# Gates of the later columns behind the fourth chunk, low words on two engines and other block sizes, in an mLSTM with a bilinear MLP

## The chip, the cores and the metric

The kernel runs on one core of a Trainium2 chip. The metric is device time in microseconds (us). Engines are named as in the profile: PE (TensorE) does matmuls, ACT (ScalarE) activations and copies, DVE (VectorE) elementwise work, POOL (GpSimd) elementwise work on SBUF, and SP (SyncE) issues all DMAs, from one queue in order.

## The reference

An mLSTM runs over 4 batches x 8 heads, 768 steps and a head dimension of 40. Its output, 3072 tokens of 320 values, goes through a bilinear MLP with d_ff = 1536. All inputs are float32 but the three MLP matrices, which are float64.

```python
for t in range(S):
    m_new = np.maximum(f_gate[:, :, t] + m, i_gate[:, :, t])
    f_stab = np.exp(f_gate[:, :, t] + m - m_new)
    i_stab = np.exp(i_gate[:, :, t] - m_new)
    m = m_new
    C = f_stab[:, :, None, None] * C + i_stab[:, :, None, None] * np.einsum('bhd,bhe->bhde', vt, kt)
    n = f_stab[:, :, None] * n + i_stab[:, :, None] * kt
    h_tilde = np.einsum('bhde,bhe->bhd', C, qt)
    denom = np.maximum(np.abs(np.einsum('bhd,bhd->bh', n, qt)[:, :, None]), 1.0)
    y[:, :, t] = 1.0 / (1.0 + np.exp(-o_gate[:, :, t])) * h_tilde / denom
x = y.transpose(0, 2, 1, 3).reshape(B * S, H * D)
out = (x @ w_a) * (x @ w_b) @ w_out
```

## The kernel before

**Chunks.** The 768 steps are cut into 6 columns of 128, and a chunk is one column of one batch: 24 chunks, ordered by column and then batch, so chunks 0 to 3 are the first column. In a chunk the recurrence becomes attention: S = k q^T per head, times a matrix E of decays (the masked exp of gate sums), times v (pV); plus, from the second column on, the state of the batch times q (pI); then a division by the denominator and a product with the output gate (stage_f), and a transpose (stage_d, `pX`) that yields x for the MLP, split into a high and a low part (`xh`, `xl`). stage_u adds the chunk's k and weighted v (`vw`, made by weigh on POOL) to the state `cst` of its batch.

**Gates.** first_gates handles the first 128 columns (chunks 0 to 3); their E comes from one-hot matmuls (begin_e). later_gates handles the other 640: a running maximum (scan, L218), three adds, a prefix sum for each column (L228), a table `tab` with three rows of columns, its write to DRAM (`g_dram`, L235), transposes on PE (`ptg`) into `gtab`, exps on ACT (L263), and `dec`, the decay from column to column. load_g reads a chunk's sums back from `g_dram`, broadcast to 128 partitions (`gbc`); stage_e masks it on POOL (L409) and takes eight exps on ACT (L416). In this kernel the weights `vw` of chunks 0 to 3, too, are read from `gtab`.

**MLP weights.** The float64 words are loaded as they are (`raw`, 32 stages), and each is turned into float32 and then into a high and a low float32r part: high on ACT (L342), low words on DVE for stages 0 to 4 and on ACT for stages 5 to 31 (L350, L352), join on DVE (L357), lead_part on ACT (L370), low_part on DVE (L376). The conversions of stages 5 to 31 run beside block 0. An up-projection step of index ff needs all stages up to 8*(ff//3)+4.

**Blocks.** The MLP runs over blocks of two or three chunks (`sizes`). Each of a block's 12 steps has 16 up matmuls (`pu`, L747), 256 or 384 wide, evacuated by ACT and DVE (L754 to L759), and, two steps later, three down matmuls a chunk (`pd`, L719). Three PSUM buffers hold `pu`. Beside block kb the attention of the next block's chunks is emitted; run_block paces it. Blocks 0 and 1 are ordered by a scheduler that simulates the engines; from block 2 on the order of PE and SP is that of the code, and the other engines are scheduled. Chunks up to 5 run as early_chunk, the later ones as late_chunk with bf16 triples and the DMA transposes of stage_a. Before block 0 a hand-written order on PE, ACT, DVE and SP does chunks 0 and 1 and stages 0 to 4.

**Loads.** SP issues q, k, v of a chunk into one of three buffers (`qk`, `va`), so chunk 3 uses the buffers of chunk 0 and has to wait for that chunk's stage_u. Each DMA also waits for the one eight issues earlier.

The rule that puts an instruction behind others is `with tc.issue_after(x)`. Three of the places that the change touches are these:

```python
        with tc.issue_after(start["dve"]):
            nc.vector.tensor_tensor_scan(m, f, i, gm[:, P - 1:P], op0=ALU.add, op1=ALU.max)
    sizes = [2, 2, 3, 3, 3, 3, 3, 2, 3]
        if x < NF0:
            nc.vector.tensor_scalar(W.bitcast(U32), lo, 2.0 ** -29, 7.0, op0=ALU.mult, op1=ALU.min)
```

## Time and profile before

| | before |
|---|---|
| median of 3 runs (lowest to highest) | 552.54 us (552.09 to 553.96) |
| profiled execution, its own time | 555.06 us |
| its span | 553.28 us |
| mean granted clock of PE | 0.975 |
| block 0's outputs copied on ACT (L729) | 102.91 us |
| block 1's | 151.41 us |
| block 2's | 211.37 us |
| HBM read / written | 41.11 / 5.97 MB |

Times within the execution count from the start of the span. A row of groups gives line, engine, operation, output <- inputs, shape, count | busy us, mean ns of one | idle time of the engine just before it and who ended most of it. A row of stretches gives, for each engine, its busy time in the stretch and (in brackets) its instructions, then the clock that was granted to PE, the mean busy share of the DMA engines, and GB/s. A row of waits reads: engine, instruction <- engine and line waited for: us in total, times, the longest. A row of the timeline has start, duration, engine, line, operation. A row of the chain of waits has start, us, engine, tile, line and count.

### The profile page before, as it was taken

The numbers are of one execution on the slowest core, as the hardware profiler recorded it, in microseconds if no ns is written. First come the engines' busy times: TensorE is split into PE (matmuls) and PEld (weight loads), VectorE is DVE, ScalarE is ACT, GpSimd is POOL, SyncE is SP. The second block draws the span as 40 slices with busy tenths as digits, with TensorE's granted clock in tenths as the row PEclk, the third lists the DMA queues.
The fourth block names the chain that finished last, engine by engine and source line by source line (L and its number), as shares of the span: only waits on it lengthen the run. The fifth ranks groups of instructions, "written<-read, shape, count | busy, mean of one in ns | idle before, by whom it ended". The sixth has DMA issues, their size and how long they took to land.

```text
span 553.3 us, 12427 instructions
## 1 busy us (share of the span) xinstructions
PE 529.7 (96%) x4810; PEld 504.1 (91%) x4810; DVE 407.9 (74%) x940; ACT 233.8 (42%) x559; POOL 126.5 (23%) x185
## 2 busy tenths in 40 slices
PE   9668999999999999999999999999999999899997
PEld 6568899998999999999899999899999999799997
DVE  6887868769799885997589895887777568744342
ACT  5699986434433451343342341542331514210111
POOL 2003534543143223133043122133030202100000
PEclk9687899999999999999999999999999999999999
DMA  9999814778639756569558564957555745100001
GB/s 174 307 253 318 146 28 101 161 139 154 109 97 186 153 95 129 107 110 188 92 130 163 117 113 122 157 104 155 84 130 78 134 77 131 21 1 25 1 0 37
DMA packets 198679, 66.77 MB, mean 121 GB/s; under 512 B 184252, under 2 KB 191900, under 8 KB 198620
## 3 DMA queue, kind: packets, MB, share of 16 engines
q1 hardware_dynamic: 198620, 65.98, 58.2%
q8 instruction: 38, 0.62, 0.5%
q14 instruction: 21, 0.17, 0.1%
HBM read 41.11 MB, written 5.97 MB: 85 GB/s over the span
## 4 chain that ended last, share of the span: by engine, by line
PE 74%; ACT 10%; DVE 5%; DMA 5%; issue 4%; SPq 2%; POOL 1%; POOLq 0%; ACTq 0%; DVEq 0%
PE pu L747 40%; PE pd L719 20%; PE pV L523 3%; DMA osig<-in_o_gate_dram 2%; PE pS L471 2%; PE pU L547 2%; ACT qks L342 1%; ACT L167 1%; ACT w L370 1%; PE pS L821 1%; PE pX L633 1%; PE pV L873 1%; SPq L160 1%; ACT cw L352 1%; ACT gbc L416 1%
## 5 line engine op out<-in xcount | busy, mean ns | idle before, releaser
L747 PE MATMUL pu<-xh,w 128*128 128x384 f32 (+1 forms) x1080 | 281.3, 327 | 2.1 <-ACT gbc L787 0.7
L747 PE MATMUL pu<-xl,w 128*128 128x384 f32 (+1 forms) x648 | 210.3, 326 | 1.0 <-DVE xl L639 1.0
L747 PEld LDWEIGHTS pu<-xh,w 128*128 128x128 f32 x1080 | 193.9, 192 | 4.0 <-ACT xh L637 1.0
L719 PE MATMUL pd<-w,gh 128*128 128x320 f32 x576 | 132.2, 316 | 2.8 <-ACT gh L757 2.8
L747 PEld LDWEIGHTS pu<-xl,w 128*128 128x128 f32 x648 | 124.6, 192 | 1.8 <-DVE xl L639 1.3
L719 PEld LDWEIGHTS pd<-w,gh 128*128 128x128 f32 x576 | 98.0, 191 | 3.5 <-ACT gh L757 3.2
L755 DVE TENSOR_TENSOR g<-pu,g 128x384 f32<-128x384 f32 (+1 forms) x108 | 54.7, 507 | 58.8 <-PE pu L747 55.5
L754 ACT COPY g<-pu 128x384 f32<-128x384 f32 (+1 forms) x92 | 40.4, 439 | 116.0 <-PE pu L747 114.7
L719 PE MATMUL pd<-w,gl 128*128 128x320 f32 x288 | 89.3, 319 | 0.0
L416 ACT ACTIVATE gbc<-gbc,gtab 128x128 f32<-128x128 f32 x160 | 49.2, 391 | 21.5 <-POOL gbc L409 19.8
L458 POOL TENSOR_TENSOR vr<-va 128x336 f32<-128x336 f32 x18 | 14.1, 782 | 188.7 <-PE pV L523 178.3
L719 PEld LDWEIGHTS pd<-w,gl 128*128 128x128 f32 x288 | 53.8, 191 | 0.2
L759 DVE TENSOR_TENSOR gl<-g,gh 128x384 fp32r<-128x384 f32 (+1 forms) x92 | 50.8, 552 | 1.6
L757 DVE CAST gh<-g 128x384 fp32r<-128x384 f32 (+1 forms) x96 | 34.2, 356 | 1.6
L478 ACT CAST pb<-gbc 128x512 bf16<-128x512 f32 x36 | 22.2, 616 | 29.4 <-DVE gbc L476 29.4
L530 DVE TENSOR_TENSOR num<-pV,num 128x336 f32<-128x336 f32 x18 | 9.1, 505 | 31.7 <-PE pV L523 31.6
L565 ACT CAST cb<-cst 128x168 bf16<-128x168 f32 x18 | 6.0, 332 | 54.5 <-DMA gbc<-g_dram 21.4
L610 POOL TENSOR_TENSOR osig<-osig,den 128x320 f32<-128x320 f32 x22 | 17.7, 804 | 41.1 <-DVE den L605 22.1
L409 POOL TENSOR_SCALAR_AFFINE_SELECT gbc<-gbc 128x1024 f32<-128x1024 f32 x20 | 23.6, 1182 | 14.6 <-DMA gbc<-g_dram 12.3
L476 DVE TENSOR_TENSOR gbc<-pS,gbc 128x512 f32<-128x512 f32 x36 | 24.5, 681 | 3.3 <-PE pS L471 3.3
L523 PEld LDWEIGHTS <-pb 128*128 128x128 bf16 x576 | 23.0, 96 | 4.1 <-DVE pb L482 1.8
L523 PE MATMUL pV<-va,pb 128*128 128x42 bf16 x288 | 25.0, 183 | 1.6 <-DVE pb L482 1.6
(131 smaller groups left out, 809.1 us busy)
## 6 DMA issues: line engine op xcount, KB each, us to landing
gbc<-g_dram SPq DMA_DIRECT2D x20, 512.0 KB
qk<-in_q_dram SPq DMA_DIRECT2D x24, 160.0 KB
qk<-in_k_dram SPq DMA_DIRECT2D x24, 160.0 KB
va<-in_v_dram SPq DMA_DIRECT2D x24, 160.0 KB
osig<-in_o_gate_dram SPq DMA_DIRECT2D x24, 160.0 KB
raw<-in_moe_w_out_dram SPq DMA_DIRECT2D x12, 320.0 KB
out_dram<-o SPq DMA_DIRECT2D x24, 160.0 KB
raw<-in_moe_w_a_dram SPq DMA_DIRECT2D x8, 384.0 KB
```

The lines of the kernel that those rows point to most:

```text
L409: nc.gpsimd.affine_select(E, E, pattern=[[0, H], [1, P]], compare_op=ALU.is_ge, fill=-1e30, base=0, channel_multiplier=-1,)
L416: nc.scalar.activation(E[:, h], E[:, h], AF.Exp, bias=beta[:, h:h + 1])
L476: nc.vector.tensor_tensor(E, pS, E, op=ALU.mult)
L478: nc.scalar.copy(pb[:, 0], E)
L523: nc.tensor.matmul(pv[:, h], pb[i][:, h % HH, :], vb[j][:, h], start=(x == 0), stop=(x == len(terms) - 1),)
L610: (nc.vector if n < NS else nc.gpsimd).tensor_tensor(yv, yv, den.unsqueeze(2).broadcast_to([P, H, D]), op=ALU.mult)
L719: nc.tensor.matmul(pd[t][:, 0:DM], a[:, cols], w, start=(ff == 0 and first), stop=(ff == NF - 1 and last),)
L747: up_in = nc.tensor.matmul(acc[j], a, r, start=(x == 0), stop=(x == len(terms) - 1),).ins
L754: (nc.vector.tensor_copy if kb > 0 and ff in [1, 2] else nc.scalar.copy)(g, acc[0])
L755: nc.vector.tensor_tensor(g, acc[1], g, op=ALU.mult)
L757: (nc.vector.tensor_copy if kb > 0 else nc.scalar.copy)(gh, g)
L759: (nc.gpsimd if kb * 12 + ff < 16 else nc.vector).tensor_tensor(gl, g, gh.bitcast(F32), op=ALU.subtract)
```

## The change

It has these parts:

- later_gates runs no longer at the start of the work beside block 0, but in early_chunk(3), behind that chunk's V, F, D and U. Its first scan follows the last low part (`after["dve"]`). It leaves out the first column, so `tab`, `gtab` and `g_dram` have five columns, and the exps of `gtab` become two.
- first_weights, new, makes the weights of chunks 0 to 3 in the hand-written part (an add on DVE, a transpose on PE, an exp on ACT into `w0tab`). weigh for chunks 0 and 1 follows there, and their stage_u comes first beside block 0.
- The low words of stages with an even number go to DVE, the odd ones stay on ACT.
- sizes is [2, 2, 2, 3, 3, 3, 3, 3, 3].
- The squash (sigmoid of the output gate) of batches 2 and 3 is emitted after the E of chunk 3. q and k of chunk 2 are loaded ahead of the weights of stages 9 to 12. The pace of run_block in block 0 has a lead of 8 units, and a conversion step is emitted every 3 units, not 4. The zeroing of `qks2` is split. The tile of `vw` shares its tag with `vr`.

```diff
+    w0tab = wpool.tile([P, BH], F32, name="w0tab")
...
-    sizes = [2, 2, 3, 3, 3, 3, 3, 2, 3]
+    sizes = [2, 2, 2, 3, 3, 3, 3, 3, 3]
...
+    def first_weights():
+        w0 = gf[:, 0:P]
+        nc.vector.tensor_scalar(w0, gb3[0][:, 1], gb3[0][:, 0, P - 1:], None, op0=ALU.add)
+        pw = ps_dn.tile([P, 512], F32, tag="pd2", name="pw")[:, 0:BH]
+        nc.tensor.transpose(pw, w0, ident[0:BH, 0:BH])
+        nc.scalar.activation(w0tab, pw, AF.Exp)
+
     def later_gates():
...
-        with tc.issue_after(start["dve"]):
+        with tc.issue_after(after["dve"]):
             nc.vector.tensor_tensor_scan(m, f, i, gm[:, P - 1:P], op0=ALU.add, op1=ALU.max)
...
-        with tc.issue_after(start["act"]):
-            nc.scalar.copy(G[:, 0], gb3[0][:, 0])
-            nc.scalar.copy(tab[BH:2 * BH, 0], gb3[0][:, 1])
...
-            nc.sync.dma_start(g_dram.rearrange("c g t -> g c t"), G)
+            nc.sync.dma_start(g_dram[1:].rearrange("c g t -> g c t"), G[:, 1:])
...
-        x = gtab[:, BH:].rearrange("p (c g) -> p c g", g=3 * BH)[:, :, 0:2 * BH]
+        nc.scalar.activation(a_col(1, 0, B), a_col(1, 0, B), AF.Exp)
+        x = gtab[:, 4 * BH:].rearrange("p (c g) -> p c g", g=3 * BH)[:, :, 0:2 * BH]
...
     def w_col(c, b):
-        return g_col(c, b, 1)
+        return g_col(c, b, 1) if c > 0 else w0tab[:, b * H:(b + 1) * H]
...
-        if x < NF0:
+        if x < NF0 or x % 2 == 0:
             nc.vector.tensor_scalar(W.bitcast(U32), lo, 2.0 ** -29, 7.0, op0=ALU.mult, op1=ALU.min)
         else:
             nc.scalar.activation(W.bitcast(U32), lo, AF.Copy, scale=7.499 * 2.0 ** -32)
...
                     high(x)
+                with tc.issue_after(start["dve" if x % 2 == 0 else "act"]):
                     low(x)
...
-        for x in qks2:
+        clear(qks2[0:2])
...
-        if n > NS:
+        if n > NS and n != NE:
             yield from stage_d(n - 1)
         aside("O", n)
+        if n == NE - 1:
+            yield from begin_c(n)
+            yield from stage_f(n)
+            yield from stage_d(n)
+            yield from stage_u(n)
+            yield from later_gates()
+            clear(qks2[2:4])
+            load_g(NE)
         yield from (begin_e if n + 1 < NE else stage_e)(n + 1)
+        if n == NS:
+            for b in range(NS, B):
+                squash(0, b, 1)
...
-        yield from begin_c(n)
-        yield from stage_u(n)
-        yield from stage_f(n)
+        if n != NE - 1:
+            yield from begin_c(n)
+            yield from stage_u(n)
+            yield from stage_f(n)
...
-        vw = apool.tile([P, H, DV], F32, tag="vw", name=f"vw{n}", bufs=1)
+        vw = apool.tile([P, H, DV], F32, tag="vr", name=f"vw{n}")
...
-        for x in range(5, 13):
+        for x in range(5, 9):
             fetch(x)
-        load(2)
+        load_qk(2)
+        for x in range(9, 13):
+            fetch(x)
+        load_v(2)
...
         run(E[1], 2)
+        first_weights()
         run(S_[1])
...
+        for n in range(NS):
+            weigh(n)
...
     def rest():
-        gates = later_gates()
-        for _ in range(2):
-            next(gates)
-            yield
-        yield from begin_a(NS)
-        yield from begin_e(NS)
-        yield from gates
         for n in range(NS):
-            weigh(n)
             yield from stage_u(n)
             if n == 0:
                 with tc.issue_after(issued["w"]):
                     load(NS + 1)
-        for b in range(2, B):
-            squash(0, b, 1)
-        load_g(NE)
+        yield from begin_a(NS)
+        yield from begin_e(NS)
         yield from attention()
...
-        acc = 0.0
+        lead_in = 8 if kb == 0 else 0
+        acc = -lead_in
...
-            if x % (4 if kb == 0 else 6) == 0:
+            if x % (3 if kb == 0 else 6) == 0:
                 next(conv, None)
-            acc += units / (total * (0.93 if kb < 2 else 0.88))
+            acc += (units + lead_in) / (total * (0.93 if kb < 2 else 0.88))
```

What the scheduler makes of it, at three places. Names carry the tile's number; the lines of the kernel after are shifted by some 5 to 25 against those before.

On ACT beside the start of block 0, before: L342 is high, L352 a low word, L370 a lead part, L754 and L757 evacuate `pu`, L787 is an exp of E, L167 the squash.

```order
L787 ACT_TABLE_LOAD
L787 ACTIVATE gbc_513<-pE_0_514 128x512
L167 ACT_TABLE_LOAD
L167 ACTIVATE osig_159<-osig_159 128x320
L787 ACT_TABLE_LOAD
L787 ACTIVATE gbc_513<-pE_1_535 128x512
L370 CAST w_588<-cw 128x384
L342 ACTIVATE qks_89<-raw_184 128x384
L167 ACT_TABLE_LOAD
L167 ACTIVATE osig_159<-osig_159 128x320
L757 CAST gh_0_502<-g_0_470 128x256
```

The same place on ACT in the changed kernel (L347 is high, L357 a low word, L375 a lead part, L775 and L778 evacuate `pu`, L808 is the exp of E, L168 the squash):

```order
L168 ACTIVATE osig_160<-osig_160 128x320
L357 ACTIVATE cw<-raw_181 128x384
L168 ACTIVATE osig_160<-osig_160 128x320
L375 CAST w_587<-cw 128x384
L347 ACTIVATE qks_89<-raw_193 128x320
L357 ACTIVATE cw<-raw_185 128x384
L778 CAST gh_1_565<-g_1_521 128x256
L775 COPY g_2_619<-pu_2_0_569 128x256
L808 ACT_TABLE_LOAD
L808 ACTIVATE gbc_604<-pE_0_605 128x512
L375 CAST w_669<-cw 64x384 x2
```

The two squashes stand ahead of the exps of E, so one table load is left of four; no further one comes until block 1.

On SP behind the last weight load, before: q of chunk 3 (`qk_80`), the write of the gate sums, then loads of chunks 3 to 5, k of chunk 3 among them, and the first `gbc`.

```order
L142 DMA qk_80<-in_q_dram 128x8x40
L235 DMA g_dram<-qks_92 32x6x128
L148 DMA va_86<-in_v_dram 128x8x40
L142 DMA qk_81<-in_q_dram 128x8x40
L142 DMA qk_80<-in_k_dram 128x8x40
L148 DMA va_87<-in_v_dram 128x8x40
L142 DMA qk_82<-in_q_dram 128x8x40
L180 DMA gbc_696<-g_dram 128x1024
```

The same place on SP in the changed kernel:

```order
L143 DMA qk_80<-in_q_dram 128x8x40
L143 DMA qk_80<-in_k_dram 128x8x40
L149 DMA va_86<-in_v_dram 128x8x40
L143 DMA qk_81<-in_q_dram 128x8x40
L149 DMA va_87<-in_v_dram 128x8x40
L143 DMA qk_82<-in_q_dram 128x8x40
L143 DMA qk_81<-in_k_dram 128x8x40
L143 DMA qk_82<-in_k_dram 128x8x40
```

k of chunk 3 follows its q. The gate sums and their first reading now stand 20 rows on, at the end of block 0, again on SP in the changed kernel (L751 writes block 0's outputs, L161 loads output gates of the second column):

```order
L240 DMA g_dram<-qks_92 32x5x128
L161 DMA osig_1475<-in_o_gate_dram 128x8x40 x2
L751 DMA out_dram<-o_0_1239 128x320
L751 DMA out_dram<-o_1_1242 128x320
L181 DMA gbc_1362<-g_dram 128x1024
L181 DMA gbc_1401<-g_dram 128x1024
```

Between the write and the first reading two loads and the two outputs of block 0 are queued.

On ACT around the exp of `gtab` (L263) and `dec` (L269), before, in the middle of block 0:

```order
L352 ACTIVATE cw<-raw_194 128x320
L263 ACT_TABLE_LOAD
L263 ACTIVATE gtab<-gtab 128x5x64
L269 ACTIVATE dec<-pdec 128x64
L352 ACTIVATE cw<-raw_198 128x384
L754 COPY g_3_742<-pu_3_0_691 128x256
```

And in the changed kernel, at the start of block 1 (L266 and L268 are the exps of `gtab`, L425 those of chunk 4's E and, in the last row, chunk 5's, L274 is `dec`):

```order
L266 ACTIVATE gtab<-gtab 128x32
L775 COPY g_0_1271<-pu_0_0_1247 128x256
L268 ACTIVATE gtab<-gtab 128x4x64
L425 ACTIVATE gbc_1362<-gbc_1362,gtab 128x128 x8
L274 ACTIVATE dec<-pdec 128x64
L168 ACT_TABLE_LOAD
L168 ACTIVATE osig_1475<-osig_1475 128x4x320
L775 COPY g_3_1410<-pu_3_0_1385 128x256
L425 ACT_TABLE_LOAD
L425 ACTIVATE gbc_1401<-gbc_1401,gtab 128x128 x8
```

The copy of block 1's fourth accumulator stands behind the exps of chunk 4's E, `dec` and the squash.

More of the change, by code (lines that the diff above doesn't have):

```diff
@@ L245, in later_gates @@
         nc.vector.tensor_tensor(
-            tab[2 * BH:], tab[BH:2 * BH], G[:, :, P - 1:P].broadcast_to([BH, NC, P]), op=ALU.add
+            tab[2 * BH:, 1:], tab[BH:2 * BH, 1:], G[:, 1:, P - 1:P].broadcast_to([BH, NC - 1, P]),
+            op=ALU.add,
         )
@@ L251, in later_gates @@
             n3 = NC // 2
-            for c in range(n3):
+            cs = range(max(half * n3, 1), (half + 1) * n3)
+            for x, c in enumerate(cs):
                 nc.tensor.transpose(
-                    pt[:, c * 3 * BH:(c + 1) * 3 * BH], tab[:, half * n3 + c, :],
-                    ident[0:3 * BH, 0:3 * BH],
-                )
-            n0, n1 = (BH, n3 * 3 * BH) if half == 0 else (0, (n3 * 3 - 1) * BH)
-            nc.vector.tensor_copy(
-                gtab[:, half * (n3 * 3 - 1) * BH:][:, 0:n1 - n0], pt[:, n0:n1]
-            )
+                    pt[:, x * 3 * BH:(x + 1) * 3 * BH], tab[:, c, :], ident[0:3 * BH, 0:3 * BH]
+                )
+            n1 = (len(cs) * 3 - half) * BH
+            nc.vector.tensor_copy(gtab[:, (3 * cs[0] - 1) * BH:][:, 0:n1], pt[:, 0:n1])
             yield
-        x = gtab[:, BH:].rearrange("p (c g) -> p c g", g=3 * BH)[:, :, 0:2 * BH]
+        nc.scalar.activation(a_col(1, 0, B), a_col(1, 0, B), AF.Exp)
+        x = gtab[:, 4 * BH:].rearrange("p (c g) -> p c g", g=3 * BH)[:, :, 0:2 * BH]
         nc.scalar.activation(x, x, AF.Exp)
@@ L270, in later_gates, with g_col @@
         yield
-    def g_col(c, b, x):
-        return gtab[:, (3 * c + x) * BH + b * H:][:, 0:H]
+    def g_col(c, b, x, nb=1):
+        return gtab[:, (3 * c + x) * BH + b * H:][:, 0:nb * H]
     def beta_col(c, b):
@@ L278, in w_col, with a_col @@
     def w_col(c, b):
-        return g_col(c, b, 1)
-    def a_col(c, b):
-        return g_col(c - 1, b, 2)
+        return g_col(c, b, 1) if c > 0 else w0tab[:, b * H:(b + 1) * H]
+    def a_col(c, b, nb=1):
+        return g_col(c - 1, b, 2, nb)
     def weight_stages():
@@ L393, in weights, with clear @@
                 yield x
-        for x in qks2:
+        clear(qks2[0:2])
+    def clear(tiles):
+        for x in tiles:
             for w in range(2):
@@ L621, in stage_d @@
     def stage_d(n):
-        s = st[n] if n < NS else st.pop(n)
+        s = st[n] if n < NE else st.pop(n)
         k_ = block[n]
```

## The prediction

> **What bounds the kernel now.** The page comes first: the busy shares and the granted clock over 40 slices of 13.8 us.
>
> ```profile
> PE 529.7 (96%) x4810; PEld 504.1 (91%) x4810; DVE 407.9 (74%) x940; ACT 233.8 (42%) x559; POOL 126.5 (23%) x185
> PEclk9687899999999999999999999999999999999999
> ```
>
> TensorE is busy for 96% of the span, so only time in which it idles or runs slowly can be won. The clock row says where the second kind lies: in the first six slices. The busy times by stretches, cut where the clock changes and where blocks end, give the sizes.
>
> ```profile
> core 0: us, PE busy (x) PEld busy (x) DVE busy (x) ACT busy (x) POOL busy (x), PEclk, DMA share, GB/s
> ...
> 22.25:71.80 49.55, 41.10 (x312) 37.69 (x313) 41.06 (x78) 46.89 (x110) 12.73 (x19) 0.78 0.93 233
> 71.80:102.90 31.10, 31.10 (x255) 29.34 (x254) 23.00 (x49) 22.22 (x57) 14.20 (x23) 1.00 0.38 79
> ...
> 102.90:151.40 48.50, 47.24 (x470) 45.28 (x470) 38.57 (x95) 19.99 (x57) 17.45 (x22) 1.00 0.76 145
> ...
> 211.40:274.30 62.90, 61.78 (x599) 58.73 (x598) 51.06 (x119) 23.53 (x58) 16.73 (x21) 1.00 0.67 131
> ...
> 456.10:500.70 44.60, 42.12 (x484) 41.16 (x483) 28.71 (x73) 11.77 (x30) 5.07 (x6) 1.00 0.20 48
> ```
>
> The first matmul of block 0 stands at 22.25 us. From there to 71.8 TensorE idles 49.55 - 41.10 = 8.45 us, and the mean clock of 0.78 takes up to 0.22 x 49.55 = 10.9 us more. After 71.8 the clock is full and TensorE has work almost without a gap. So 8.45 + 10.9 = 19.3 us is about all that this change can touch before the later blocks. Who holds TensorE there? ACT is busy 46.89 of 49.55 us. The waits of TensorE name ACT's casts and a load:
>
> ```profile
> PE pd L719 <- ACT gh L757: 2.8, 2, 1.7
> PE pT L808 <- DMA qk<-in_q_dram: 2.5, 1, 2.5
> ```
>
> ACT's groups while the weights of stages 5 to 31 are converted, 25.8 to 89.4 us, show what fills it.
>
> ```profile
> L370 ACT CAST w<-cw 128x384 fp32r<-128x384 f32 (+2 forms) x31 | 15.6, 502 | 4.6 <-DVE cw L357 4.5
> ...
> L352 ACT ACTIVATE cw<-raw 128x384 uint32<-128x384 uint32 (+1 forms) x27 | 14.0, 532 | 0.0
> ...
> L787 ACT ACT_TABLE_LOAD x2 | 2.6, 1283 | 0.0
> L167 ACT ACT_TABLE_LOAD x2 | 2.6, 1283 | 0.0
> L416 ACT ACTIVATE gbc<-gbc,gtab 128x128 f32<-128x128 f32 x8 | 2.5, 430 | 0.0
> ```
>
> **The change, part by part.** ACT first. 13 of the 27 low words leave it: 13 x 0.532 = 6.9 us. Five table loads stand in this stretch (two and two above, one for gtab's exps) and by the new order one is left: 4 x 1.28 = 5.1 us. The exps of chunk 4 (2.5 us) and the gates' small copies and exps (1.3 us) move behind the stretch. ACT's durations overlap by about a fifth where they stand side by side (the groups add up to 71 us in 58 us of busy time), so 10.7 us of ordinary work is worth 8.7, and with the loads 13.8 us. ACT idles 5.5 us there. Without idle time its last cast comes at 89.4 - 5.5 - 13.8 = 70 us instead of 89.4.
>
> VectorE takes the 13 low words and loses the gates.
>
> ```profile
> L376 DVE TENSOR_TENSOR w<-cw,w 128x384 fp32r<-128x384 f32 (+2 forms) x29 | 17.5, 618 | 1.3 <-ACT w L370 1.0
> L357 DVE SCALAR_TENSOR_TENSOR cw<-qks,cw 128x384 uint32<-128x384 uint32 (+1 forms) x27 | 16.8, 644 | 1.5 <-ACT cw L352 1.0
> ...
> L228 DVE TENSOR_TENSOR_SCAN qks<-one,qks 32x128 f32<-32x128 f32 x5 | 1.7, 389 | 0.0
> L218 DVE TENSOR_TENSOR_SCAN qks<-qks 32x640 f32<-32x640 f32 x1 | 1.5, 1542 | 0.0
> ...
> L222 DVE TENSOR_TENSOR qks<-qks 32x640 f32<-32x640 f32 x1 | 0.8, 815 | 0.0
> ```
>
> ```profile
> 22.29 0.36 DVE L350 TENSOR_SCALAR cw<-raw 128x384 uint32<-128x384 uint32 x1
> ```
>
> 13 x 0.36 = 4.7 us come. The gates go: 1.7 + 1.5 + five operations of 0.8 to 0.95 and two copies of 0.4, 8.1 us; with them some 3 us of chunk 4's attention. VectorE idles 13.5 us in the stretch now, so without idle time it would be through at 89.4 - 13.5 - 8.1 - 3 + 4.7 = 69.5 us. Both engines thus end near 70, each nearly full. Weights of the last up-projection steps are wanted three stages (5 us) earlier.
>
> Now TensorE. I follow the end T of block 0's last up-projection.
>
> ```profile
> 99.47 0.28 PE L747 MATMUL pu<-xl,w 128*128 128x256 f32 x1
> ```
>
> T is 99.75 before. The new order has less ahead of that point: chunk 4's S, I and transposes, the gate transposes, a chunk's U and X and 12 down matmuls come later. From the groups of TensorE, 22 to 102 us, and its pitch in the chain of waits:
>
> ```profile
> L821 PE MATMUL pS<-T,T 40*128 40x128 f32 x48 | 5.8, 285 | 0.0
> L808 PE MATMUL pT<-ident,qk 128*128 128x128 f32 x32 | 5.3, 293 | 2.6 <-DMA qk<-in_q_dram 2.5 <-DMA qk<-in_k_dram 0.2
> ...
> L547 PE MATMUL pU<-vw,qk 128*64 128x42 f32 x84 | 4.1, 249 | 0.0
> ...
> L842 PE MATMUL pI<-cst,T 40*128 40x42 f32 x16 | 2.2, 284 | 0.0
> ```
>
> ```profile
> 493.30 1.92 PE pu L747 x16
> ...
> 498.02 2.64 PE pd L719 x18
> ```
>
> A third of 5.8, three eighths of 5.3, a quarter of 4.1, all of 2.2, about 2 for gate transposes and X, and 12 x 0.147 = 1.8: 11 us, some 9.5 where the records' overlaps are taken off. This work is not saved, only done later. At equal work T before is 99.75 - 9.5 = 90.2 us.
>
> When does T come after? From TensorE: 77.5 us from 22.25 to T are 8.45 idle, 10.9 clock and 58.2 work; less 9.5 leaves 48.7. With half the clock loss (5.5) and a wait of 2 us for chunk 2's q, whose load moves ahead of five weight loads, T = 22.25 + 48.7 + 5.5 + 2 = 78.4. From the loads of chunk 3:
>
> ```profile
> 49.55 0.38 SPq L142 DMA_DIRECT2D qk<-in_q_dram  x1
> ```
>
> ```profile
> 56.72 0.68 SPq L142 DMA_DIRECT2D qk<-in_k_dram  x1
> ```
>
> ```profile
> 61.54 0.66 PE L808 MATMUL pT<-ident,qk 128*128 128x128 f32 x4 [0.16 <-DMA qk<-in_k_dram]
> ```
>
> k is issued at 56.72 and lands by 61.5; in the new queue it follows q at once, since U of chunk 0 no longer waits for the gate table, so about 51.7 and landed by 56.5. Behind its transposes stand 81 up matmuls of 0.12, 30 down of 0.147, two V (3.8), S, U and X (3): 21 us, T = 77.5 at full clock and 79.5 with one more slow stretch. I take **T = 79: a gain of 11.2 us**. Bounds: 76 if everything keeps pace, 85 if ACT and VectorE wait for each other at every stage.
>
> Then the gates, now ahead of chunk 4. The scan waits for the last low part; by VectorE's new order the five chunk scans come right behind the product of the last up step, at T + 2.4. SP's order is g_dram, two gate loads, block 0's two outputs, then chunk 4's gbc.
>
> ```profile
> 26.54 1.54 DVE L218 TENSOR_TENSOR_SCAN qks<-qks 32x640 f32<-32x640 f32 x1
> ```
>
> ```profile
> 51.79 0.43 SPq L235 DMA_DIRECT2D g_dram<-qks  x1
> ...
> 59.88 0.98 SPq L180 DMA_DIRECT2D gbc<-g_dram  x1
> ...
> 83.31 0.36 SPq L180 DMA_DIRECT2D gbc<-g_dram  x1
> ```
>
> ```profile
> 65.49 1.31 POOL L409 TENSOR_SCALAR_AFFINE_SELECT gbc<-gbc 128x1024 f32<-128x1024 f32 x1 [1.26 <-DMA gbc<-g_dram]
> ...
> 87.42 1.10 POOL L409 TENSOR_SCALAR_AFFINE_SELECT gbc<-gbc 128x1024 f32<-128x1024 f32 x1 [0.79 <-DMA gbc<-g_dram]
> ```
>
> ```profile
> 101.73 1.27 ACT L167 ACTIVATE osig<-osig 128x1280 f32<-128x1280 f32 x1
> ```
>
> Block 0's last 18 down matmuls, X and transposes end at T + 3.8, the outputs are issued at T + 5, gbc at T + 6.3. It lands after 4.1 us (83.31 to 87.42; 5.6 from 59.88), the mask takes 1.2, the exps 2.5: T + 14.2. ACT is in order: dec's exp, a table load of 1.28, the squash of 1.27 and only then the copy of pu of step 3, done at T + 17.3. TensorE reaches the matmul that needs this accumulator (64 + 8 up, 12 down, 3 us of small work) at T + 16.5. I charge **1.2 us**, between 0 (block 0's tail slower than that) and 11 (a rival below). E itself is wanted only some 8 us later, so the rest of the chain is covered; uncovered, its 14 us would count whole.
>
> Block sizes: matmul counts stay (three blocks of 2, six of 3). Three late chunks beside a block of 2 now fall to block 2. VectorE has 51.06 us in a full block, about 6 less beside a block of 2, 45 us, where such a block takes 44.6. I charge **1.0 us** (0 to 3). Block 7 is no longer such a block, and block 1 gets two chunks; their idle 1.3 and up to 2.5 us (some of it missing records) I credit with **0.5** (0 to 2). first_weights adds a small transpose, an add and an exp ahead of 22.25, beside idle time of TensorE: nothing, 0.4 at most. vw of chunks 0 to 3 runs on POOL earlier: nothing, since POOL is busy 12.73 of 49.55 us; its cover gone, 1.1 each.
>
> Sum: -11.2 + 1.2 + 1.0 - 0.5 = **-9.5 us**. The profiled execution took 555.06 us (span 553.28), 2.5 above the median of 552.54; its like would be 545.6, and the median 552.5 - 9.5 = **543.0 us**.
>
> **The clock.** The slow stretches are no plain answer to idling:
>
> ```profile
> 47.90:65.00 17.10, 14.56 (x148) 12.91 (x146) 14.97 (x27) 17.02 (x42) 5.99 (x8) 1.00 0.94 213
> 65.00:71.80 6.80, 6.80 (x40) 6.38 (x41) 5.98 (x14) 6.61 (x21) 3.97 (x5) 0.50 0.56 90
> ```
>
> Before 65.0 TensorE was 85% busy, and still the next 6.8 us ran at half clock. Hence I keep half the clock loss though the idle gaps shrink. The Trainium skill ("TensorE: Matmul & The Clock Gate", Part 1: The HAM clock gate) has the clock halved after an idle window of about 3.4 us and released after a busy one. By that rule a well-fed block 0 would run at full clock from about 31 us on. The trace agrees in the length of the stretches (6.8 is two such windows), not in the cause at 65.0.
>
> **The rivals.**
> - *The clock stays open after 31 us*: loss 4.3 instead of 5.5 and no second slow stretch behind k; T = 76.3, sum -12.2, **540**. For: fewer gaps. Against: the row at 65.0. 13%.
> - *VectorE becomes the bound of block 0*. Each stage goes ACT, VectorE, ACT, VectorE; joins and low parts took 0.62 to 0.64 us, over the 0.5 of their quick ones. If half of its 13.5 us of idle time stays, the last cast is at 76.5 and T near 83.5: sum -5, **547.5**. 17%.
> - *The gain is given back in blocks 1 and 2* by charges at their upper ends (some 4 + 3) on top of T = 83.5: **552**. 5%.
> - *Slower: the gate chain is exposed.* Before, scan to mask took 65.49 - 26.54 = 39 us, for gbc stood behind other loads. Starting at T - 7 and 3.8 us from mask to E, it would end at T + 36, where TensorE wants E at T + 24.8: 11 us of stall, and two slow windows (3.4): -11.2 + 11 + 3.4 + 1 - 0.5 = +3.7, **556**. It decides from a stall of 8 us. Against: its queue place is now close behind g_dram. 5%.
>
> **How the numbers follow.** The forecast (540.5 to 546) has 60%. The range of 538 to 550 takes in the first two rivals and leaves out 10 to 15%. A measurement of this kernel tells 0.3%, 1.7 us, from no change. Faster: 60 + 13 + 17 = 90%; same 5%; slower 5%.
>
> **What would show it.** Right: block 0's outputs copied on ACT near 84 us instead of 102.9; one table load for L787 there; the last weight cast near 70; a wait of about 1 us of TensorE for the copy of pu in block 1. Wrong: VectorE above 95% to 80 us with TensorE waiting for w; a PE wait for E of chunk 4; idle time of several us in block 2.

## The result, and the profile after

The kernel after takes 567.23 us (564.30 to 569.63, 4 executions) against 552.54: ratio 1.026, 95% interval 1.021 to 1.031. It is slower by 2.6%, where 543.0 us, faster by 1.7%, was forecast, and it lies outside the range of 538 to 550. The profiled execution took 566.81 us (span 565.0), so it stands for the median.

The first view is the page of the kernel after: TensorE's busy share, and the granted clock in 40 slices, here of 14.1 us.

```profile
PE 532.7 (94%) x4810; PEld 503.4 (89%) x4810; DVE 411.9 (73%) x954; ACT 224.1 (40%) x542; POOL 128.2 (23%) x185
PEclk9699899999899799999999999999999899999999
```

The share fell from 96% to 94%. Of the 6, 8, 7 and 8 in slices two to five a 6 and an 8 are left, as hoped, but there are new dents in slices eleven, fourteen and thirty-two, where the kernel before had none. The stretches say which blocks they are in (block 0 in three pieces, block 1, block 2, block 6; columns as in the prediction):

```profile
22.25:58.40 36.15, 29.19 (x254) 25.83 (x255) 28.75 (x60) 30.84 (x77) 5.78 (x7) 0.92 1.04 270
58.40:61.80 3.40, 3.40 (x18) 3.40 (x17) 1.03 (x2) 1.81 (x5) 2.05 (x3) 0.50 1.11 147
61.80:88.66 26.86, 25.07 (x202) 23.63 (x201) 25.70 (x56) 16.09 (x43) 10.16 (x16) 1.00 0.35 55
88.66:146.16 57.50, 54.11 (x449) 49.74 (x448) 40.10 (x92) 24.50 (x66) 20.32 (x29) 0.98 0.52 110
146.16:201.88 55.72, 48.50 (x560) 46.05 (x560) 46.68 (x118) 22.21 (x59) 16.53 (x21) 0.93 0.82 152
...
388.39:453.24 64.85, 62.51 (x583) 59.67 (x582) 51.76 (x122) 23.24 (x57) 14.12 (x17) 0.97 0.66 125
```

Block 0 ends at 88.66 instead of 102.91. Block 2 takes 55.72 us with 55.72 - 48.50 = 7.2 us of idle TensorE and a mean clock of 0.93: less what the half clock takes, 2.5 us, its matmuls need 46. That is the loss the eye finds first. TensorE's waits in that block:

```profile
PE pX L642 <- DVE qks L454: 3.3, 1, 3.3
PE pV L532 <- DVE pb L491: 2.3, 2, 1.3
```

The longer one lies at the block's end. These are the instructions there: the transposes (`pX`) of chunk 7, the load of the third column's output gates on SP, and then the chain of waits.

```profile
174.54 0.49 PE L642 MATMUL pX<-ident,osig 128*128 128x128 f32 x3
```

```profile
182.38 3.14 SPq L161 DMA_DIRECT2D osig<-in_o_gate_dram  x4
```

```profile
188.80 0.34 ACT g L775
189.15 0.02 issue
189.17 1.28 ACT L168
190.45 0.01 issue
190.46 1.27 ACT osig L168
191.73 0.52 ACT pb L487
...
193.00 0.48 DVE osig L622
...
194.72 0.12 DVE osig L624
194.84 0.04 issue
194.88 0.47 PE pX L642
```

Chunk 8 is the first of a column. There is one tile of output gates, so their load has to wait for chunk 7's transposes and for its turn on SP, which comes 7 us after them; behind it stand a table load, the squash, a product on POOL, VectorE's product and copy, and only then chunk 8's transposes, which end the work beside block 2. In the chain above the table load follows a copy on ACT at once, so the squash's place in ACT's order counts as well as the load. TensorE takes its work in the order of the code here: it stands still for 3.3 us, and 191.5 to 198.3 runs at half clock. (The row of waits names L454 as releaser; the chain shows the copy L624 ending just ahead of `pX`.)

The dent in slice thirty-two is the same thing once more. Chunk 20 also starts a column and is the last one beside block 6, which idles 2.3 us and loses 1.7 to the clock; in the kernel before, where chunks 19 and 20 alone stand beside it, block 6 lost nothing. Its one wait in the kernel after:

```profile
PE pX L642 <- DVE osig L622: 2.3, 1, 2.3
```

### The profile page after: what moved, and what is told of

Read it like the earlier page. It is cut to its first block, busy times and chain, and to the rows that moved or that the text cites. A ratio compares the mean times of both kernels' runs of the same rounds, so it can differ in the third digit from the quotient of the medians.

```text
span 565.0 us, 12428 instructions
## 1 busy us (share of the span) xinstructions
PE 532.7 (94%) x4810; PEld 503.4 (89%) x4810; DVE 411.9 (73%) x954; ACT 224.1 (40%) x542; POOL 128.2 (23%) x185
## 3 DMA queue, kind: packets, MB, share of 16 engines
q1 hardware_dynamic: 198588, 65.96, 58.3%
## 4 chain that ended last, share of the span: by engine, by line
PE 64%; DMA 10%; DVE 10%; SPq 6%; ACT 4%; issue 4%; POOL 1%; POOLq 0%; DVEq 0%; ACTq 0%
PE pu L768 36%; PE pd L740 18%; DMA qk<-in_q_dram 4%; PE pV L532 3%; DMA raw<-in_moe_w_b_dram 3%; SPq L336 2%; PE pS L480 2%; DMA osig<-in_o_gate_dram 1%; PE pU L556 1%; SPq L161 1%; DMA qks<-in_f_gate_dram 1%; PE pX L642 1%; DVE w L381 1%; ACT osig L168 1%; ACT L168 1%
## 5 line engine op out<-in xcount | busy, mean ns | idle before, releaser
L776 DVE TENSOR_TENSOR g<-pu,g 128x384 f32<-128x384 f32 (+1 forms) x108 | 54.7, 506 | 65.2 <-PE pu L768 58.7
L775 ACT COPY g<-pu 128x384 f32<-128x384 f32 (+1 forms) x92 | 40.3, 440 | 119.7 <-PE pu L768 117.7
L425 ACT ACTIVATE gbc<-gbc,gtab 128x128 f32<-128x128 f32 x160 | 49.1, 389 | 18.6 <-POOL gbc L418 18.6
L778 DVE CAST gh<-g 128x384 fp32r<-128x384 f32 (+1 forms) x96 | 33.9, 353 | 1.6
L418 POOL TENSOR_SCALAR_AFFINE_SELECT gbc<-gbc 128x1024 f32<-128x1024 f32 x20 | 22.9, 1144 | 18.4 <-DMA gbc<-g_dram 14.9
L489 DVE TENSOR_TENSOR gbc<-gbc,pb 128x512 f32<-128x512 f32 x36 | 25.3, 701 | 1.4 <-ACT pb L487 1.4
```

What stands on the lines that cost most here:

```text
L418: nc.gpsimd.affine_select(E, E, pattern=[[0, H], [1, P]], compare_op=ALU.is_ge, fill=-1e30, base=0, channel_multiplier=-1,)
L425: nc.scalar.activation(E[:, h], E[:, h], AF.Exp, bias=beta[:, h:h + 1])
L489: nc.vector.tensor_tensor(E, E, pb[:, 0], op=ALU.subtract)
L775: (nc.vector.tensor_copy if kb > 0 and ff in [1, 2] else nc.scalar.copy)(g, acc[0])
L776: nc.vector.tensor_tensor(g, acc[1], g, op=ALU.mult)
L778: (nc.vector.tensor_copy if kb > 0 else nc.scalar.copy)(gh, g)
```

## Experiments

Times are medians; the ratio is to the kernel before in the same comparison, with its 95% interval. The last three columns are where ACT first copies the outputs of blocks 0, 1 and 2 in the profiled execution, in us.

| run | what it is | us | ratio | b0 | b1 | b2 |
|---|---|---|---|---|---|---|
| before | | 552.5 | 1 | 102.9 | 151.4 | 211.4 |
| after | | 567.2 | 1.026 (1.021-1.031) | 88.7 | 146.2 | 201.9 |
| e1 | after, old sizes | 555.6 | 1.004 (1.002-1.006) | 85.6 | 147.3 | 211.4 |
| e2 | before, new sizes | 563.7 | 1.018 (1.015-1.020) | 100.8 | 142.9 | 197.3 |
| e3 | after, gl on POOL in block 2 | 568.5 | 1.027 (1.022-1.032) | 87.0 | 144.0 | 202.0 |
| e4 | after, low words on ACT | 567.9 | 1.025 (1.021-1.029) | 93.2 | 145.5 | 203.1 |
| e5 | e1, first scan early | 557.2 | 1.007 (1.004-1.011) | 92.1 | 150.7 | 210.5 |
| e6 | e1, all gates early | 557.9 | 1.008 (1.005-1.011) | 93.9 | 152.2 | 212.5 |
| e7 | after, output gates by batch | 565.1 | 1.022 (1.017-1.027) | 87.8 | 143.0 | 197.7 |
| e8 | e1, output gates by batch | 559.8 | 1.011 (1.006-1.015) | 87.5 | 155.8 | 214.1 |
| e9 | after, no gl in block 2 | 565.8 | 1.022 (1.017-1.026) | 87.8 | 146.0 | 201.2 |
| e10 | after, gh on ACT in block 2 | 566.5 | 1.024 (1.020-1.028) | 85.8 | 145.8 | 204.3 |
| e11 | after, two-chunk block 4 | 571.3 | 1.031 (1.026-1.036) | 89.0 | 150.1 | 214.5 |
| e12 | before, two chunks last | 555.3 | 1.004 (1.002-1.007) | 101.0 | 149.6 | 210.2 |
| e13 | e1, block 0 runs ahead | 558.1 | 1.010 (1.007-1.013) | 91.9 | 157.3 | 217.1 |
| e14 | after, block 0 runs ahead | 567.6 | 1.025 (1.020-1.029) | 87.6 | 143.5 | 199.2 |
| e15 | after, two-chunk block 3 | 562.3 | 1.018 (1.014-1.022) | 85.1 | 146.9 | 204.5 |
| e16 | before, low words split | 554.9 | 1.003 (1.001-1.005) | 97.0 | 149.4 | 209.7 |
| e17 | before, again | 552.9 | 1.001 (0.999-1.003) | 99.9 | 148.5 | 208.4 |
| e18 | e1, faster pace in block 1 | 557.5 | 1.007 (1.005-1.010) | 89.5 | 151.5 | 215.9 |

Block 2 has two chunks in after, e2, e3, e4, e7, e9, e10 and e14 and three in the others, so the last column compares only within each group.

### Is it the sizes?

e1, and e2 the other way round in the kernel before:

```diff
-    sizes = [2, 2, 2, 3, 3, 3, 3, 3, 3]
+    sizes = [2, 2, 3, 3, 3, 3, 3, 2, 3]
```

> The kernel after with the block sizes of before, [2, 2, 3, 3, 3, 3, 3, 2, 3]. Theory A (three late chunks beside the two-chunk block 2 keep VectorE behind: block 2 took 55.7 us where its matmuls need about 45): the some 10 us of block 2 and the 2 to 3 of blocks 6 and 7 go; block 1 takes over the sixth chunk (4 us of matmuls) as before, so about 552, 549 to 555. Rival B (the gate chain at the start of block 1 is what costs): block 1 is the dense one now, on top of the gates, and the loss stays: 560 or more. Rival C (low words on VectorE and block 0 cost it): unchanged within 2 us, 565 to 569.

> The kernel before with the block sizes of after and nothing else. Theory A: block 2 gets the same three late chunks beside 256-column matmuls, so slower by about 9 to 12 us, 561 to 565, with block 2 near 55 us and TensorE idle some 6 us in it. Rivals B and C: the sizes are nearly free, 551 to 554.

e1 measured 555.6, 11.6 us under the kernel after; e2 measured 563.7, 10 us over the kernel before. Theory A's numbers hold in e2 and miss e1's upper end by 0.6. Most of the loss is thus the sizes, whatever else is changed. Block 2 of e2 shows the same picture (7.5 us idle, clock 0.94), with the same two waits of 3.3 and 2.2 us, and in its block 6 TensorE waits 3.6 us for `pX`:

```profile
142.94:197.27 54.33, 46.81 (x545) 44.16 (x545) 45.95 (x116) 21.38 (x57) 16.58 (x21) 0.94 0.76 143
```

But e1 is still 2 us behind the kernel before, where the rest of the change was to win 10 by the prediction's sum. So there are two questions: what happens in a two-chunk block, and where the gain of block 0 went.

### What holds a two-chunk block with three late chunks?

VectorE's load first, in three ways. `gh` and `gl` are the high and the low part of a block's product `g`. e3 gives the subtractions that make `gl` in block 2 to POOL, e9 leaves them out (block 2's outputs then lack the low part), and e10 gives the casts that make `gh` to ACT:

```diff
-            (nc.gpsimd if kb * 12 + ff < 16 else nc.vector).tensor_tensor(
+            (nc.gpsimd if kb * 12 + ff < 16 or kb == 2 else nc.vector).tensor_tensor(
```

```diff
+            if kb == 2:
+                gs[ff] = (gh, gh)
+                return
```

```diff
-            (nc.vector.tensor_copy if kb > 0 else nc.scalar.copy)(gh, g)
+            (nc.vector.tensor_copy if kb > 0 and kb != 2 else nc.scalar.copy)(gh, g)
```

(e10 also puts the two early copies of `g` in block 2 on ACT.)

> The kernel after with the 12 subtractions that make gl in block 2 on POOL instead of VectorE (about 12 x 0.35 = 4 us off VectorE there, POOL is busy 16.5 of 55.7 us). Theory A (VectorE's load is the bound of block 2): 4 to 8 us faster than the kernel after, 559 to 563. Rival D (a late load of q and the order of SP's queue hold block 2): within 2 us of it, 565 to 569. If POOL's slower subtraction delays the down matmuls, slower.

> The kernel after, leaving out the 12 subtractions for gl in block 2 (gh is used in its place, so block 2's outputs lack the low part): 12 x 0.418 = 5.0 us less for VectorE there and nothing added to POOL, the matmuls stay. Theory A (VectorE's load bounds block 2): block 2 takes 49 to 52 us instead of 55.7, total 559 to 564. Rival H (a late chunk takes some 16 us of chained steps whatever the load, so three of them and a tail take 55): unchanged, 565 to 569.

> The kernel after with the casts to gh and the two early copies of g in block 2 on ACT (12 x 0.28 and 2 x 0.42 = 4.2 us off VectorE; ACT is busy 22 of 55.7 us there). Theory A: block 2 takes 50 to 53 us, total 560 to 565. Rival H: unchanged, 565 to 569. If ACT's order puts the casts behind exps and squash: 567 or more.

All three lie outside theory A's ranges: 568.5, 565.8 and 566.5. In e9 block 2 took 55.2 us though VectorE's work there fell from 46.7 to 41.9. Its two waits say why: the one for VectorE's `pb` halved, the one at the end stayed.

```profile
PE pX L642 <- DVE qks L454: 3.4, 1, 3.4
PE pV L532 <- DVE pb L491: 1.1, 2, 0.6
```

So VectorE's load is a part, at most some 1 us, and not what sets the block's end. In e10 block 2 even took 58.4 us, though VectorE's work fell to 43.9: the wait at the end grew to 3.8. e3 was no clean test (block 2 took 58.0); the last section tells why.

Then the output gates (e7, and e8 with the old sizes): one tile a batch, so that three of the four are loaded and squashed a chunk earlier.

```diff
-            osig[c] = apool.tile([P, B, 3 * P], F32, tag="osig", name=f"osig{c}", bufs=1)
+        osig[c, b] = apool.tile([P, 3 * P], F32, tag=f"osig{b}", name=f"osig{c}_{b}", bufs=1)
...
-        if o == "O" and n % B == 0 and n > 0:
-            load_o(n // B)
+        if o == "O" and n == B:
+            load_o(1)
+        if o == "O" and n > B and n % B == B - 1 and n + 1 < NCH:
+            load_o(n // B + 1, 0, B - 1)
+        if o == "O" and n > B and n % B == 0:
+            load_o(n // B, B - 1, B)
```

> The kernel after with one tile of output gates per batch instead of one for all four, so that batches 0 to 2 of the next column are loaded and squashed beside the last chunk of the column before, and only batch 3 beside its first chunk. Theory F (at the end of block 2 chunk 8 is the first of a column: its load of output gates waits for chunk 7's transposes, then table load, squash and product stand in a row ahead of the last transposes; 4 us idle and 3.4 us of half clock in 188 to 198; the same in block 6 with chunk 20): block 2 takes 49 to 52 us instead of 55.7, block 6 loses less too, total 557 to 562. Rival D (load of VectorE or the queue order alone): 565 to 569.

> The same split of the output gates on e1. With the old sizes chunk 8 is in the middle of its block's work and chunks 12 and 20 are last beside blocks that wait about 1 us or less. Theory F: the order of chunks hid the chain there, so 0 to 2 us faster than e1, 553.5 to 556. If the chain mattered with any sizes: 551 or less. If the four shorter squashes and the added table loads cost: 557 or more.

e7: 565.1, above theory F's range and at the lower edge of rival D's. The waits of its block 2:

```profile
PE pu L772 <- ACT g L779: 4.1, 2, 2.9
PE pV L532 <- DVE pb L491: 1.6, 2, 1.2
```

The wait for `pX` is gone, as theory F has it, but a new one for a copy of `pu` has come, 2.9 us at its longest. ACT's timeline in e7 (L168 the squash, L779 the copy) shows what stands ahead of that copy:

```profile
171.12 2.45 ACT L425 ACTIVATE gbc<-gbc,gtab 128x128 f32<-128x128 f32 x8
173.59 1.28 ACT L168 ACT_TABLE_LOAD   x1
174.88 0.83 ACT L168 ACTIVATE osig<-osig 128x320 f32<-128x320 f32 x2
175.62 0.35 ACT L779 COPY g<-pu 128x256 f32<-128x256 f32 x1
```

The moved squash and its table load delay the copy; block 2 took 54.7. Block 6 got worse: TensorE waits 5.4 us there for the same copy, where it waited 2.3 for `pX` in the kernel after. e8, with the old sizes, is 4 us slower than e1; its profile idles as long as e1's up to the last block's end (18.5 against 18.4 us) and loses 9.5 against 5.0 us to the clock, for a reason that wasn't followed. The chain is real, but this way round it is no cure.

Last, a two-chunk block elsewhere (e11, e15):

```diff
-    sizes = [2, 2, 2, 3, 3, 3, 3, 3, 3]
+    sizes = [2, 2, 3, 3, 2, 3, 3, 3, 3]
```

```diff
-    sizes = [2, 2, 2, 3, 3, 3, 3, 3, 3]
+    sizes = [2, 2, 3, 2, 3, 3, 3, 3, 3]
```

> The kernel after with the sizes [2, 2, 3, 3, 2, 3, 3, 3, 3]: the two-chunk block that has three late chunks with state beside it is block 4 (chunks 12 to 14), where no output gates are loaded for the last of them. Theories A and H: block 4 takes 54 to 57 us where its matmuls need about 46, total 564 to 569. Rival S (it was special to block 2: the column that starts with its last chunk, the first late chunks): block 4 takes 46 to 49, total 555 to 560.

> The kernel after with the sizes [2, 2, 3, 2, 3, 3, 3, 3, 3]: the two-chunk block that has three late chunks beside it is block 3, with chunks 9 to 11, among which no column starts. Theory F (the output gates of a column that starts there cost some 4.5 us of idle time and the half clock behind it, the rest is VectorE and the pace of the chunks): block 3 takes 49 to 52 us, total 559 to 564. Rival H (three late chunks need 54 to 58 us of chained steps in any case): block 3 takes 54 to 58 us, total 564 to 570 as with e11.

e11 measured 571.3, above both ranges. In it chunk 12, which starts a column, is beside the two-chunk block: 58.3 us, 8.6 idle, a wait of 4.6 for `pX`. That the column's start was spared there was an error in the expectation; it had only moved from the last chunk to the first. In e15 no column starts beside the block:

```profile
204.49:257.81 53.32, 48.73 (x566) 46.07 (x565) 45.36 (x119) 20.90 (x57) 16.03 (x21) 0.97 0.73 142
```

```profile
PE pV L532 <- DVE pb L491: 2.4, 2, 1.6
PE pX L642 <- DVE gbc L485: 1.2, 1, 1.2
```

53.3 us with 4.6 idle, and 562.3 in all, 5 less than after. By the block's length a column's start is worth 2.4 us (55.7 to 53.3); by idle time and lost clock it is 3.5 (9.8 to 6.3). Either is an estimate, since block 3 has other chunks beside it and each kernel has one profile. What is left is TensorE's wait for VectorE's `pb` and products, 3.6 of the 4.6 us in the two rows, and the clock behind it; that these waits come from three chunks' steps beside two chunks' matmuls is argued, not shown. Theory F's total holds, its 49 to 52 for the block doesn't. What would be left with both causes removed at once wasn't tried.

e12 put the two chunks last in the kernel before:

> The kernel before with the sizes [2, 2, 3, 3, 3, 3, 3, 3, 2], so that no two-chunk block but block 1 has three chunks beside it (block 7 of before, with three chunks of the last column, idled 2.5 us in 45). Theory A: 549 to 553, at best 2.5 us faster than before. If the last two-chunk block alone runs its matmuls with more gaps: 553 to 556.

555.3: the 2.5 us of idle time in block 7 of the kernel before weren't to be had this way. Block 7 no longer idles, but block 6 does, 2.8 us, in waits for `pX`.

### Where did block 0's gain go?

e16 makes the split of the low words, and nothing else, in the kernel before; e4 undoes it in the kernel after (the same lines the other way round):

```diff
-        if x < NF0:
+        if x < NF0 or x % 2 == 0:
             nc.vector.tensor_scalar(W.bitcast(U32), lo, 2.0 ** -29, 7.0, op0=ALU.mult, op1=ALU.min)
...
+                with tc.issue_after(start["dve" if x % 2 == 0 else "act"]):
                     low(x)
```

> The kernel after with all low words of stages 5 to 31 on ACT again (27 instead of 14). Theory A (the split helps block 0 and has nothing to do with the loss): block 0 ends 2 to 6 us later than 88.7, total 569 to 573. Rival C (VectorE with the low words is what was lost in block 0 and behind): block 0 no later, total 567 or less. If block 0 is held by the load of chunk 3's q alone, no change of either.

> The kernel before with the low words of even stages on VectorE and nothing else. ACT was busy 46.9 of 49.6 us in 22 to 72 and loses 13 x 0.53 = 6.9 us; VectorE gains 13 x 0.36 = 4.7. If ACT holds block 0 by itself: the last cast at about 82 instead of 89.4, block 0's end 3 to 6 us earlier, total 547 to 550. If VectorE, the loads of chunk 3 or the half clock take it back: 551 to 554.

In e4 block 0 ends 4.5 us later, and block 1 at the same time (145.5 against 146.2); the total is the same, between the two ranges. e16 is slower by 0.3%, above both of its ranges, though its block 0 ends 3 to 6 us earlier. An earlier end of block 0 is no gain by itself.

Theory G held the late gates responsible (in e1, e5 moves the scan, e6 all of later_gates with the reading of the sums to the start of the work beside block 0; e5's edit is shown):

```diff
-        with tc.issue_after(after["dve"]):
+        with tc.issue_after(start["dve"]):
             nc.vector.tensor_tensor_scan(m, f, i, gm[:, P - 1:P], op0=ALU.add, op1=ALU.max)
```

> e1 (the kernel after with the old sizes, 555.6 us) with the first scan of the later gates behind the hand-written part instead of behind the last low part, so that VectorE makes the scans beside the conversions of block 0. Theory G (the gate chain, not the load of block 1, starves VectorE at the start of block 1 - busy 2.3 and 2.1 us of 5 there in e1 - and the debt shows as idle time and half clock at block 1's end): block 0 ends up to 4 us later than 85.6, E of chunk 4 some 5 us earlier than 95.5, block 1 ends at 142 to 146 instead of 147.9, total 549 to 553. Rival L (block 1 has too much work for VectorE wherever the gates stand): block 1's end and the total do not move, 554 to 558.

> e1 with the whole of the later gates emitted at the start of the work beside block 0, as in the kernel before (scan, sums, write, table, load of chunk 4's sums). Theory G: block 0 ends later, at 90 to 96, but block 1 has E of chunk 4 at its start and ends at 144 to 149 without idle time at its end; total 548 to 553, that is what the low words and the load order bring alone. Rival L: block 1 still ends with 3 us or more of idle time, 554 to 558.

Both miss theory G's ranges: 557.2 and 557.9, no better than e1. The end of block 1 did improve, from 4.8 us idle to 2.6 and 2.5, but block 0 ended 6 and 8 us later. And the starved start was no such thing: in the kernel before, too, VectorE is busy only 8.4 of the first 15 us of block 1.

Theory U: block 0 stops handing out attention work when chunk 3's transposes are emitted, which is now after 33 units instead of 55; block 1 has to place the rest. e13 and e14 let block 0 go on to 55, e18 only raises block 1's pace:

```diff
-                done = r is not None and r[1] >= last
+                given += 1
+                done = given >= 55 if kb == 0 else r is not None and r[1] >= last
-        while not done:
+        while not done and kb > 0:
```

```diff
-        units = (36 if kb < 2 else STEPS) * sizes[kb + 1] if kb + 1 < NB else 1
+        units = (36 if kb < 1 else 43 if kb < 2 else STEPS) * sizes[kb + 1] if kb + 1 < NB else 1
```

> e1 (after with the old sizes, 555.6 us) with block 0 handing out attention work up to 55 units, as many as in the kernel before, instead of stopping at 33 with the transposes of chunk 3. Theory U (block 1 ends with work that has no matmuls left beside it): block 1 ends without its 4.8 us of idle time and 1.6 us of half clock, at 141 to 145 instead of 147.9; block 0's end moves back some 3 to 7 us; total 547 to 552. Rival L (VectorE's load in block 1 is the bound whatever the order): 554 to 558.

> The same on the kernel after with its own sizes (567.2 us). Theory U: block 1 loses its 3 us of idle time and 1 us of half clock, block 2 still takes 54 to 58 us; total 561 to 565. Rival L: 566 to 569.

> e1 (after with the old sizes, 555.6 us) with block 1 handing out its attention work at a pace of 129 units instead of 108, since it has 119 to place; block 0 is left as it is. Theory U: block 1 ends with 1 to 2.5 us of idle time instead of 4.8 and without half clock behind it, total 550 to 553. Rival L (VectorE's load): 554 to 557.

e13 took the idle time in block 1 from 4.8 to 1.6 us, as expected, and was still at 558.1: in its profile, the slowest of its executions (561.0), blocks 0 and 1 lost it to the clock (0.89 and 0.91). e14's executions reach from 562.6 to 570.0, too wide to tell. e18 (557.5) kept its 4.7 us of idle time: the pace is not it. In e1 the end of block 1 looks like this:

```profile
85.62:139.60 53.98, 52.96 (x520) 49.96 (x519) 41.42 (x98) 25.24 (x69) 24.93 (x35) 1.00 0.72 148
139.60:147.93 8.33, 4.55 (x31) 3.30 (x30) 8.33 (x21) 4.99 (x14) 0.85 (x2) 0.74 0.59 113
```

VectorE is busy in all of the last 8.33 us while TensorE does 4.55. Block 1's stretch in e1 has 49.8 us of VectorE's work, where the same block of the kernel before has 38.6: the 11 us that block 0 was relieved of. But the load alone doesn't make the idle time: e13 has 47.4 us of it in block 1 and idles 1.6. Where the work stands among the matmuls counts too.

### How much was there to win?

> The kernel before, unchanged, profiled once more. If the half clock at 65.0 to 71.8, behind a full stretch, is chance: it is not there, or elsewhere, and block 2's outputs are copied 2 to 4 us earlier than 211.4 unless another such stretch takes its place; then some 3 us of the gap that the prediction counted on belonged to that execution. If it belongs to the kernel: it stands within 3 us of the same place.

The second profile of the kernel before:

```profile
65.00:71.80 6.80, 6.80 (x63) 6.29 (x64) 6.43 (x15) 6.80 (x22) 3.99 (x5) 1.00 0.64 87
99.86:148.50 48.64, 47.38 (x471) 45.31 (x471) 38.67 (x95) 19.98 (x58) 17.47 (x22) 1.00 0.77 144
148.50:208.44 59.94, 59.14 (x577) 56.06 (x576) 50.89 (x117) 23.80 (x56) 16.54 (x21) 1.00 0.71 130
```

The half clock at 65.0 to 71.8 was chance: it isn't here, nor in e2 and e12, whose instructions have the same order up to there. Without it every later block ends 3 us earlier, and the span is 550.0 instead of 553.3. What the first profile showed as block 0's gap was 2 to 3 us more than the other three have (block 0 ends at 102.9, and at 99.9 to 101.0).

Now old-size kernels can be compared up to the end of block 2, for from there on they take the same: 341.9 us before, 341.6 before again, 341.5 in e1 (span less block 2's end). From 22.25 us to that end, summed over stretches of half a microsecond (lost clock is busy time times one less the granted clock):

| | idle | lost clock | other busy time |
|---|---|---|---|
| before | 10.6 | 10.3 | 168.3 |
| before, again | 10.7 | 6.5 | 169.0 |
| e1 | 13.7 | 5.0 | 170.5 |
| e6 | 10.7 | 8.3 | 171.2 |
| e16 | 9.3 | 7.2 | 171.0 |

Against the second profile e1 wins 1.5 us of clock, loses 3.0 of idle time and 1.5 of busy time. 0.8 us of the loss is the start, 0.5 as idle time and 0.3 as busy time: block 0's first matmul stands at 22.75 in e1 and at 21.91 in the second profile of before. The other 1.1 to 1.2 us of busy time stay unexplained; e16 has 2.0 us more of it than the second profile. The profiles thus give +3, the medians +2.

The same sums say where e1's gain goes. At equal work of TensorE it is 6.7 us ahead of the second profile at the end of block 0's last up-projection, 5.2 ahead at block 0's end, 0.5 ahead at block 1's, and behind by 1.8 at block 2's; the unexplained busy time makes it 2.9.

## Why the prediction was wrong, step by step

The forecast was -9.5 us, the result +14.7. Two parts of the sum failed, each by some 10 us. The sizes cost 10 to 12 instead of 1.0, and the rest of the change, counted as a gain of 10.0, lost 2 to 3. Either one alone would have taken all of the forecast gain, within 2 us.

- **Block sizes, charged 1.0 (0 to 3): measured 10 to 12.** This step failed, and it turns a loss of 2 to 3 us into one of 14.7. It compared VectorE's busy time, 45 us, with block 7's 44.6 and took that block for "such a block". Block 7 of the kernel before has the last column's chunks beside it: no states to add to, no output gates to load, 28.7 us of VectorE. I had quoted that row and used only its length. A mean load says little about waits: with 41.9 us of VectorE's work (e9) the block still took 55.2. TensorE waits for single steps of a chain that crosses SP, ACT, VectorE and TensorE, and the place of the column's start among the chunks wasn't looked at. Block 2 lost 9.8 us to idle time and clock and block 6 another 4.0; that a block beside three full chunks could also lose was not in the sum. The sign for it, "idle time of several us in block 2", was on the list and came.
- **T = 79, a gain of 11.2: T came at 83.1, a gain of about 7 at equal work, of which 2 to 3 were chance.** The term that failed is the wait, 2 us: TensorE idled 7.3 us from 22.25 to T. In the eight profiles whose block 0 has this same order (after, e1, e3, e9, e10, e11, e15, e18) it idled 5.4 to 7.8, and T came at 79.5 to 84.0. The last weight cast ended at 78.6, not near 70, since ACT idled 11.2 us up to it, 6.1 of them in waits for VectorE's joins; no idle time was the assumption. Up to 60 us the loads held things up too (DMA share 1.04). q of chunk 3 took 8.5 us:

```profile
49.01 0.38 SPq L143 DMA_DIRECT2D qk<-in_q_dram  x1
```

```profile
57.53 0.66 PE L829 MATMUL pT<-ident,qk 128*128 128x128 f32 x4 [3.36 <-DMA qk<-in_q_dram]
```

  The bounds of 76 to 85 held it. The sum's base was wrong too: 3.4 us of the 10.9 for the clock stood in one execution only, and I had said myself that no idle time explained that stretch. And T before, 99.75, was read from a matmul of block 1. Block 0's last up matmul, the 192nd of 12 steps of 16, ends at 96.05, and VectorE starts the last product at once:

```profile
96.18 0.42 DVE L755 TENSOR_TENSOR g<-pu,g 128x256 f32<-128x256 f32 x1
```

  That the equal-work figure of 90.2 holds nevertheless is luck: up to the true T, TensorE has only 5.5 us less work, not 9.5, and 96.05 - 5.5 is 90.5.
- **"This work is not saved, only done later"**: applied to TensorE alone. VectorE's 8.1 and 3 us were credited to block 0 and charged nowhere. They fall into block 1, whose end they hold up: 4.8 us idle in e1 against 1.3. That they do was shown by moving them (e5, e6); that the exact price is VectorE's load and not the order is argued from the rows above, not shown, and e13 speaks for the order as well.
- **The gates, charged 1.2: some 2.5.** The price came from another place than the one charged. TensorE's wait for the copy of `pu` in block 1 was 0.2 us, and its wait ahead of `ptg` 0.8. But the gates' operations on VectorE, 640 wide, also stand between the last products of block 0:

```profile
82.73 1.25 DVE L230 TENSOR_TENSOR qks<-qks 32x640 f32<-32x640 f32 x1
...
84.53 1.16 DVE L229 TENSOR_TENSOR qks<-qks 32x640 f32<-32x640 f32 x1
85.62 0.41 DVE L776 TENSOR_TENSOR g<-pu,g 128x256 f32<-128x256 f32 x1
```

```profile
84.99 0.85 PE L740 MATMUL pd<-w,gh 128*128 128x320 f32 x4 [0.99 <-ACT gh L778]
86.33 0.57 PE L740 MATMUL pd<-w,gl 128*128 128x320 f32 x2 [0.50 <-POOL gl L780]
```

  The last product starts 2.5 us after T, and TensorE idles 1.5 us between T and the end of block 0; in e5 and e6, with the gates early, and in both profiles of before it idles 0.0 there. The rest of the gate chain is hidden, and the rival "gate chain exposed" didn't come.
- **Block 7 and block 1 no longer dense, credited 0.5**: block 7 idles 0.7 us instead of 2.5, but block 6 lost the 4.0 above. e12 showed no gain either.
- **first_weights, nothing to 0.4**: block 0's first matmul stands at 22.3 to 22.8 us in the eight profiles and at 21.9 to 22.3 in the four with before's order, so it starts some 0.5 us later. Which part of the change does that wasn't tested.
- The clock: up to T its loss fell from 10.3 to 4.1 us (5.5 was forecast); in the four and the eight profiles it lies at 5.2 to 10.3 and at 2.0 to 5.9. New half clock came behind the new idle gaps at the ends of blocks 1, 2 and 6.

No version beat the kernel before. The smallest part, the split of the low words, was slower by itself (1.003).

## What to carry to other kernels

Work that leaves a crowded stage is charged on every engine to the stage that receives it, not only on the bounding one. When the shape of a stage changes, its price is taken from a stage with the same neighbours: the same engines' work beside it, the same loads and column starts, not only the same size. And before a gap is counted as winnable, profile the kernel a second time: what stands in one execution only can't be won.
